# Transformer block on one core: banks, weight loads and the first cycle of a hand-written order

## The chip, the core and the metric

One core of a Trainium2 chip runs the whole program. Five engines work side by side, each through its own list of instructions in order: TensorE (PE, matmuls), VectorE (DVE), ScalarE (ACT), GpSimd (POOL) and SyncE (SP), which in this kernel only issues DMA transfers. ACT and POOL issue a few transfers too. The metric is the device time of one execution in microseconds (us). Before the change it is 1957.61 us, the median of three runs (1957.44 to 1958.38).

## The reference

The input x has 2048 tokens of 512 numbers. Two branches work on its layer norm, and their sum is added to x:

```python
def _A_ref(x, wqkv, wo):          # 32 heads of 16
    qkv = (x @ wqkv).reshape(B, S, 3, H, Dh).transpose(2, 0, 3, 1, 4)
    q, k, v = qkv[0], qkv[1], qkv[2]
    scores = jnp.einsum("bhqd,bhkd->bhqk", q, k) * (Dh ** -0.5)
    p = _softmax(scores, axis=-1)
    o = jnp.einsum("bhqk,bhkd->bhqd", p, v)
    return o.transpose(0, 2, 1, 3).reshape(B, S, D) @ wo

def _B_ref(x, w_in, w_sp, b_sp, w_out):     # F = 1792, Fh = 896
    z = _gelu(jnp.einsum("bsd,df->bsf", x, w_in))
    z1 = z[..., :Fh]
    z2 = _layernorm(z[..., Fh:], axis=-1)
    g = jnp.einsum("ts,bsf->btf", w_sp, z2) + b_sp[None, :, None]
    return jnp.einsum("bsf,fd->bsd", z1 * g, w_out)

xn = _layernorm(x)
return x + _A_ref(xn, A_wqkv, A_wo) + _B_ref(xn, B_w_in, B_w_sp, B_b_sp, B_w_out)
```

## The kernel before

**Two streams in one order.** The attention runs in 1024 steps: 16 pairs of heads, for each pair 4 chunks of 512 queries (c), for each chunk 16 tiles of 128 keys. Step n makes the scores of two heads (`scores`, L960, tile st), their exponential on ACT (`exp`, tile pf) and the product of the exponentials with v (`pv`, L934, tile o, one accumulator per chunk). 27 steps ahead of it (LEAD), the same products with the operands exchanged (`max_mm`, L650, tile mx) are reduced on DVE to row maxima (`max_red`, L658), which `max_fin` puts, through a small DRAM tile (mscr), into spare rows of the stacked q, so that the scores come out shifted. The dense products stand between: q and k of the later heads (`qk_group`), z2 (`z2_all`), z1 (`z1_all`), the spatial product (`spatial`), the output of the MLP (`mlp_out`) and of the attention (`attn_out`). Each dense matmul is done as three fp32r products of high and low parts (`mm3`, L170 to L172), so 12 of them make one product with four blocks of 128 in depth.

**The order is written by the loop at L995.** It records the instructions of all engines in program order, and no scheduler moves them. One turn is a *half*; an even half takes two steps, an odd one takes one, so two halves are a cycle of three steps. Halves below 0 hold maxima alone. In each half it records mx and st, exponentials, o products (in even halves), reductions, then one step of each generator in `bg` (loads and splits of weights) and in `side` (splits of results, the gelu and norm of z2 and z1), and last dense products from `queue`, as many as `credit` allows. Before half 0 the credit is 2600 in every half, four blocks, one product; from half 0 on it is paced by what is left to do, and only odd halves get any. `now[0]` is the half; `pool[0]` and `load` are the program's own estimate of when POOL is free and of how much ACT and DVE have.

**PSUM has eight banks.** st, mx and, at the end, al share three pairs of banks in turn (`spsum`, tags s0, s1, s2). Two single banks remain (`dpsum`): tag d (bank 7) for dense products and tag o (bank 0) for the accumulator of o. As long as no o is open, dense products may use both. In `qk_group` (L301) the two products of a call, q and k, take d and o alternately while `now[0] < -2`. A matmul that begins in a bank waits until the copy out of that bank by ACT or DVE is done: `qr` for products of q and k, `e` for o, `vall` for v.

**What follows a product of q and k.** ACT copies it out (qr), ACT makes the high part and POOL the low part (`qk_split`, tile qkhl, three buffers), and SP stores the pair of 512 KB (qscr, kscr). `load_stacks` reads them back in the layout of the scores. The normalised x (xnT) is stored too (xscr) and fetched again, group by group of 512 tokens.

**Weights of q and k.** `prepare` (L200) loads a raw tile of fp32 (three raw buffers), waits two halves, lets POOL make the parts, and only then hands them over. Heads come in four groups m of eight. The weights of m = 1 are loaded by hand at L898 to L903; those of m = 2 and 3 by `qk_prepare`, which is put into `bg` at L913, after the stacks of the first pair.

**The end.** The last pair of heads is not stored and read back like the others. `chunk_out` (L982) copies the accumulator of chunk c to SBUF (e), and `last_pair` (L776) brings values and sums of its heads into one bank (nd) with small matmuls against selector columns. For chunks 0 to 2 ACT copies nd to SBUF (L793) and `last_factors` divides there (reciprocal on DVE, product on POOL); for chunk 3 DVE divides from the bank. `last_mm` (L806) multiplies the result with the last rows of wo, two tiles of 128 tokens at a time into one pair of banks (al), and `last_add` (L814) adds that to the rest (fin, into which L772 had added the other heads' product, ao) and stores it. The last chunk's four tiles are tokens 12 to 15.

Of the kernel before, what the change touches and what calls it, by code (L numbers as in the profile page):

```python
# [16 lines left out]
P = 128  # L17
# [23 lines left out]
def fused_block(ctx, tc, x, wqkv, wo, w_in, w_spT, b_sp, w_out, out):  # L41
# [11 lines left out]

    load = {"A": 0.0, "D": 0.0}

    def act(out, in_, func, n, **kw):
        load["A"] += 0.16 + n / 1400.0
        return nc.scalar.activation(out, in_, func, **kw)  # L58

    def dve(n, rate=1):  # L60
        load["D"] += 0.065 + n / (960.0 * rate)
        return nc.vector
# [63 lines left out]
    def later(k, fn, *args):  # L126
        late.append((now[0] + k, fn, args))
# [93 lines left out]
    def prime():  # L221

        next(queue[1])
# [76 lines left out]

    def qk_group(m, g, w, tags=("d",)):  # L301
        for a in range(2):
            if now[0] < -2 and m:
                tags = ("d", "o")
            acc = dpsum(f"qk{m}_{a}_{g}", tags[a % len(tags)], ND)
            for c in range(ND):
                t = xnT[g, c]
                mm3(acc, w[a][:, 0, c * P:(c + 1) * P], w[a][:, 1, c * P:(c + 1) * P], t[:, 0, :], t[:, 1, :], c == 0, c == ND - 1)
                yield 650 + 0.5 * (c == ND - 1)
            if m == 0:  # L310
                run(qk_split(m, g, a, acc))
# [20 lines left out]
    def qk_prepare():  # L332
        yield from prepare(wq, [((m, a), *qk_weights(m, a)) for m in (2, 3) for a in range(2)])
# [81 lines left out]

    def z2_all():
        ws = w2
        def fetch(t):
            xt = piece(f"xt{t}")
            for c in range(ND):  # L420
                move(xt[:, :, c * P:(c + 1) * P], xscr[t // 4][c][:, :, (t % 4) * P:(t % 4 + 1) * P])
            return xt

        nxt = [fetch(0), fetch(1)]
        freed = []
        yield -3
        while len(ws) < 2 * ND:
            yield -1.5
        for t in range(NT):
            xt = nxt.pop(0)  # L430
            if t + 2 < NT:
                nxt.append(fetch(t + 2))
            if t == NT - 2:
                prime()
                freed.append(now[0])
                bg.append(prepare(w1, [(f, f"w1_{f}", w_in[:, f * P:(f + 1) * P], D, ND) for f in range(NF)], freed))
            z = piece(f"z2_{t}").bitcast(F32).rearrange("p a b -> p (a b)")
            for j in range(2):
# [337 lines left out]
    def last_pair(c, e):  # L776


        ones = sel["ones"]
        two = piece(f"on{c}").bitcast(F32)  # L780
        rec, on = two[:, 0, 0:P], two[:, 1, 0:P]
        acc = dpsum(f"nd{c}")
        for k in (1, 0):
            for u in range(4):
                nc.tensor.matmul(acc[32 * u:32 * u + 32, k * P:(k + 1) * P], ones[:, 0, 32 * k:32 * k + 32], e[:, u * P:(u + 1) * P], start=True, stop=True)
        yield 500.5
        if c == NG - 1:
            nc.vector.reciprocal(rec, acc[:, P:2 * P])
            nc.vector.tensor_mul(on, acc[:, 0:P], rec)
            turn.extend((4 * c + 2 * a, on) for a in range(2))  # L790
        else:
            cp = two[:, 0, P:3 * P]
            act(cp, acc[:, :2 * P], AF.Copy, 2 * P)  # L793
            bg.append(last_factors(c, cp, rec, on))
        yield 0
# [9 lines left out]

    def last_mm(t, on):  # L806

        acc = spsum(f"al{t}")
        for a in range(2):
            u = slice(32 * (t % 4 + a), 32 * (t % 4 + a) + 32)  # L810
            nc.tensor.matmul(acc[:, a, :], on[u, :], sel["ones"][u, 1, :], start=True, stop=True)
        return t, acc

    def last_add(t, acc):  # L814
        f = fin[t // 2]
        if t < NT - 2:
            dve(1024).tensor_add(f, acc, f)
            move(out[t * P:(t + 2) * P, :].rearrange("(a p) d -> p a d", p=P), f)
            return
        for a in range(2):  # L820
            dve(512).tensor_add(f[:, a, :], acc[:, a, :], f[:, a, :])
            move(out[(t + a) * P:(t + a + 1) * P, :], f[:, a, :])

    def vpack(t, h):
# [15 lines left out]
    with tc.manual_schedule(engines=engines):  # L840
# [46 lines left out]
        for g in range(NG):  # L887
            once = True
            for y in qk_group(0, g, w0, ("d", "o")):
                if y == 0 and once and g < 2:  # L890
                    once = False
                    if g == 0:
                        turn_x(1)
                        norm = norm_x(2)
                    else:
                        next(norm)
            load_stacks(0, slice(g * 512, (g + 1) * 512))
            if g == NG - 2:  # L898
                for a in range(2):
                    wq[1, a] = begin(*qk_weights(1, a))  # L900
            if g == NG - 1:
                for a in range(2):
                    wq[1, a] = end(wq[1, a])  # L903
            for t in range(4 * g, 4 * g + 4) if g else ():
                next(norm, 0)
                if t % 4 == 2:
                    if g + 1 < NG:
                        turn_x(g + 1)
                    if g + 2 < NG:
                        norm = norm_x(g + 2)  # L910
                v_tile(t, wv)
        steady.append(True)
        bg.append(qk_prepare())  # L913
        queue.extend([qk_rest(), z2_all(), z1_all(), spatial(), mlp_out(), attn_out()])
        todo = 650 * (3 * 32 + 112 + 112 + 28 * 16 + 112)
        pause = 0
# [64 lines left out]

        def chunk_out(p, c):  # L982
            e = t512(f"e{p}_{c}")
            act(e, accs.pop((p, c)), AF.Copy, 512)
            if p == NP - 1:
                later(2, lambda: urgent.append(last_pair(c, e)))
                return
            i = (p % 4) * 2
            later(1, move, escr[p // 4][c][i:i + 2].rearrange("j r w d q -> (j r w d) q"), e)
            if p % 4 == 3 or p == NP - 2:  # L990
                later(2, lambda: bg.append(norm_out(p // 4, c)))
# [3 lines left out]
        for half in range(-2 * LEAD // 3, 2 * (N // 3 + 4)):  # L995
# [3 lines left out]
            if b + LEAD >= NSTEP:  # L999
                ns = [n for n in range(b, b + 3) if n < N] if half % 2 == 0 else []  # L1000
            now[0] = half
            flush()
            for n in ns:
                if n == 16:
# [7 lines left out]
            tiles = [(scores, n) for n in ns]  # L1012
            for i, m in enumerate(ms):
                tiles.insert(1 if half % 2 == 0 else 2 * i, (max_mm, m))
            for make, n in tiles:
                make(n)
            while ended:
# [15 lines left out]
            for m in ms:  # L1033
                max_red(m)

            if half % 2 == 0:
                for m in range(ms[0] - 2, ms[0] + 1):
                    max_fin(m)
            if drain:
                drain = False  # L1040
                cost = next(queue[0], None)
                if cost is None:
                    queue.pop(0)
                else:
                    pause = -cost
            bg[:] = [g for g in bg if next(g, 0) is None]
            side[:] = [g for g in side if load["D"] > limit or next(g, 0) is None]
            ready += len(ns)
            if b < 0:
                credit = 2600  # L1050
            elif half % 2:
                credit = min(credit + 3 * (max(todo / max(DENSE - b, 10), 600 if b > DENSE - 15 else 0) if todo > 0 else max((todo + 64 * 650) / max(N - 6 - b, 8), 450)), 3250)
            else:
                continue
# [55 lines left out]
```

## Time and profile before

| | |
|---|---|
| runs, median (lowest to highest) | 1957.61 us (1957.44 to 1958.38) |
| profiled execution, its own time | 1957.17 us |
| its span, first to last instruction | 1955.4 us |
| granted TensorE clock | 0.999 |
| PE, DVE, ACT, POOL busy | 99%, 70%, 63%, 37% of the span |

In the rows of the timeline the first number is the start in us from the start of the span, the second the duration in us, then engine, line and operation, `written<-read` by the tiles' names without numbers, how many instructions are merged in the row (x4), and in brackets how long the engine was idle before and what released it. Matmuls are pipelined: a row's duration reaches past the start of the next one, so what PE spends on a matmul is read from start to start. `PEld` is the loading of weights, `SPq` the issue of a transfer by SP. A row of the waits has engine, line and what it waited for, then us in total, how many times, and the longest.

### The profile page before, as it was taken

How to read it: one execution, taken by the hardware profiler on the slowest of the kernel's cores; microseconds unless marked ns; L12 is line 12 of the kernel's file. 1: busy time of each engine (PE TensorE's matmuls, PEld its weight loads, DVE VectorE, ACT ScalarE, POOL GpSimd, SP SyncE). 2: the span in 40 equal slices, each digit the busy share in tenths (PEclk: the TensorE clock that was granted, in tenths of full speed). 3: DMA queues.
4: the chain of work that ended last, by engine and by line, in shares of the span. 5: the costliest groups of instructions: out<-in, count | busy, mean ns of one | idle time of the engine just before them, and what ended most of it. 6: DMA issues, size and time to landing. Idle time of an engine off the chain costs nothing.

```text
span 1955.4 us, 32643 instructions
## 1 busy us (share of the span) xinstructions
PE 1936.4 (99%) x12559; PEld 1050.4 (54%) x12559; DVE 1374.0 (70%) x1565; ACT 1231.1 (63%) x1407; POOL 725.1 (37%) x790
## 2 busy tenths in 40 slices
PE   9999999999999999999999999999999999999998
PEld 7765555555555555555555555555555555555543
DVE  5367777777677677777777777777777777777873
ACT  5346678888677666656666666566666655556664
POOL 3334278889776931126122531017112300002100
PEclk9999999999999999999999999999999999999999
DMA  7566344363535545365545745346454645355323
GB/s 275 198 220 182 99 115 124 114 170 114 141 130 157 181 117 139 109 154 167 137 138 166 200 134 132 104 121 205 111 156 143 174 142 136 112 145 162 105 74 113
DMA packets 229218, 284.23 MB, mean 145 GB/s; under 512 B 35192, under 2 KB 134152, under 8 KB 226184
## 3 DMA queue, kind: packets, MB, share of 16 engines
q1 hardware_dynamic: 217256, 272.64, 48.4%
q0 software_dynamic: 2592, 8.46, 1.1%
q10 hardware_dynamic: 9216, 1.05, 0.4%
q8 instruction: 99, 1.62, 0.3%
q14 instruction: 55, 0.45, 0.1%
HBM read 188.51 MB, written 93.58 MB: 144 GB/s over the span
## 4 chain that ended last, share of the span: by engine, by line
PE 93%; DVE 2%; ACT 2%; DMA 1%; issue 1%; SPq 0%; POOL 0%; DVEq 0%; ACTq 0%
PE o L934 23%; PE mx L650 16%; PE st L960 15%; PE sp L170 7%; PE sp L171 5%; PE sp L172 5%; PE qk L170 2%; PE z1p L170 2%; PE mo L170 2%; PE z2p L170 2%; PE qk L171 1%; PE qk L172 1%; PE z1p L172 1%; PE z1p L171 1%; PE mo L171 1%; PE mo L172 1%
## 5 line engine op out<-in xcount | busy, mean ns | idle before, releaser
L658 DVE TENSOR_REDUCE mm<-mx 128x2 f32<-128x1024 f32 x1024 | 1222.1, 1222 | 498.2 <-PE mx L650 493.9
L58 ACT ACTIVATE pf<-st 128x1024 f32<-128x1024 f32 x1024 | 1027.7, 1025 | 622.5 <-PE st L960 587.4
L934 PE MATMUL o<-pf,vall 128*32 128x512 f32 (+1 forms) x5120 | 511.0, 514 | 0.0
L650 PE MATMUL mx<-kst,qst 48*128 48x512 f32 x2048 | 447.5, 435 | 2.7 <-ACT pf L58 1.8
L960 PE MATMUL st<-qst,kst 50*128 50x512 f32 x2048 | 443.8, 431 | 1.3 <-DVE mm L658 1.0
L650 PEld LDWEIGHTS mx<-kst,qst 48*128 48x128 f32 x2048 | 192.2, 185 | 268.3 <-ACT pf L58 169.6
L960 PEld LDWEIGHTS st<-qst,kst 50*128 50x128 f32 x2048 | 193.2, 185 | 158.9 <-issue 85.6
L934 PEld LDWEIGHTS o<-pf,vall 128*32 128x32 f32 x5120 | 131.5, 109 | 233.3 <-issue 211.4
L170 PE MATMUL sp<-wsp,zs 128*128 128x512 f32 x448 | 194.2, 433 | 0.3 <-DVE z1i L566 0.2
L573 POOL TENSOR_TENSOR z1i<-z1i,hhl 128x512 f32<-128x512 f32 x28 | 36.0, 1286 | 413.9 <-DVE z1i L566 411.5
L171 PE MATMUL sp<-wsp,zs 128*128 128x512 f32 x448 | 176.1, 393 | 0.0
L172 PE MATMUL sp<-wsp,zs 128*128 128x512 f32 x448 | 175.8, 392 | 0.0
L170 PEld LDWEIGHTS sp<-wsp,zs 128*128 128x128 f32 x448 | 83.9, 187 | 69.4 <-issue 52.6
L172 PEld LDWEIGHTS sp<-wsp,zs 128*128 128x128 f32 x448 | 84.2, 188 | 19.5
L171 PEld LDWEIGHTS sp<-wsp,zs 128*128 128x128 f32 x448 | 84.4, 188 | 12.1
L196 POOL CAST wo<-wo0r 128x512 fp32r<-128x512 f32 x1 | 0.6, 611 | 190.1 <-DMA wo0r<-in_wo 190.1
L325 POOL TENSOR_TENSOR qkhl<-qr,qkhl 128x512 fp32r<-128x512 f32 x24 | 30.9, 1289 | 71.4 <-ACT qkhl L58 71.4
L170 PE MATMUL z2p<-w,xt 128*128 128x448 f32 x128 | 51.3, 401 | 0.0
L170 PE MATMUL mo<-wout,hp 128*128 128x512 f32 x112 | 48.6, 434 | 0.6 <-DVE xr L610 0.4
L711 POOL TENSOR_TENSOR ob<-ob 128x512 f32<-128x512 f32 (+1 forms) x16 | 20.6, 1289 | 75.6 <-DMA ob<-rscr 67.7
L172 PE MATMUL z2p<-w,xt 128*128 128x448 f32 x128 | 46.9, 366 | 0.0
L171 PE MATMUL z2p<-w,xt 128*128 128x448 f32 x128 | 46.7, 365 | 0.0
(382 smaller groups left out, 1985.2 us busy)
## 6 DMA issues: line engine op xcount, KB each, us to landing
zs<-z2scr SPq DMA_DIRECT2D x112, 512.0 KB
escr<-e SPq DMA_DIRECT2D x60, 256.0 KB
hscr<-hhl SPq DMA_DIRECT2D x28, 512.0 KB
xscr<-xnT POOLq DMA_DIRECT2D x16, 512.0 KB, 4.8
qscr<-qkhl SPq DMA_DIRECT2D x16, 512.0 KB
kscr<-qkhl SPq DMA_DIRECT2D x16, 512.0 KB
xt<-xscr SPq DMA_DIRECT2D x64, 128.0 KB
z2scr<-z2hl SPq DMA_DIRECT2D x32, 256.0 KB
```

The source lines that it names most:

```text
L58: return nc.scalar.activation(out, in_, func, **kw)
L170: nc.tensor.matmul(acc, lh, rh, start=first, stop=False)
L171: nc.tensor.matmul(acc, ll, rh, start=False, stop=False)
L172: nc.tensor.matmul(acc, lh, rl, start=False, stop=last)
L196: gps(0.6).tensor_copy(t[:, 0, :n], rw[:, :n])
L325: gps(1.3).tensor_sub(hl[:, 1 - a, :], src, hl[:, a, :].bitcast(F32))
L573: gps(1.3).tensor_add(z1, z1, hl[:, 1, :].bitcast(F32))
L650: nc.tensor.matmul(acc[:, j, :], qst[p % 2][rows, tt * P:(tt + 1) * P], kst[p % 2][rows, kc * 512:(kc + 1) * 512], start=True, stop=True)
L658: dve(1024).tensor_reduce(mmax[i // 16][:, :, t, kc], mstep.pop(i), AX.X, ALU.max)
L711: gps(1.3).tensor_mul(both[rows, 0, :], both[rows, 0, :], both[rows, 2, :])
L934: nc.tensor.matmul(acc[cols:cols + VW, a:a + w], vpack(kt - 1 + r, 2 * p + j), pf[:, j * 512 + a:j * 512 + a + w], start=(kt == 1 and a == ...
L960: nc.tensor.matmul(st[:, j, :], kst[p % 2][rows, kt * P:(kt + 1) * P], qst[p % 2][rows, c * 512:(c + 1) * 512], start=True, stop=True)
```

## The change

It has five parts.

1. **Weights.** In the last of the four turns that prepare the first pair, three steps of `qk_prepare` are taken before `load_stacks`, with the clock of halves set back by two, and three more after the last v products, with POOL's estimate reset. So loads of the weights of m = 2 and 3 are issued ahead of the last stacks, and their splits stand on POOL ahead of everything that the loop records. The generator then goes to `bg` as before.
2. **Banks of q and k.** Up to half 0, `qk_group` takes one tag for a product: o in even halves, d in odd ones.
3. **First cycle.** In the two halves of the first cycle with scores (b == 0, no o product done when the half began) the credit is 2600 as in the halves before it.
4. **Small steps on ACT.** While z2 is made (`wide` is set until its last tiles), a half in which ACT has been given more than 1.9 us by the program's estimate takes no step of `side`, unless three generators stand there. `max_fin` moves behind the queue's pending step, but only where no maxima are left, so it records nothing there.
5. **The end.** Chunk 2 is divided from its bank as chunk 3 is. The copy of the last accumulator is made in two halves of 256, ACT's and DVE's, into two tiles. The four last tiles of tokens take a bank each (two of the pairs' and banks d and o), and are added and stored one by one.

```diff
@@ def act
         load["A"] += 0.16 + n / 1400.0
+        given[0] += 0.16 + n / 1400.0
@@ def qk_group
         for a in range(2):
-            if now[0] < -2 and m:
-                tags = ("d", "o")
+            if now[0] <= 0 and m:
+                tags = ("do"[now[0] % 2 == 0],)
             acc = dpsum(f"qk{m}_{a}_{g}", tags[a % len(tags)], ND)
@@ def z2_all
         ws = w2
+        wide.append(1)
...
             if t == NT - 2:
+                wide.clear()
                 prime()
@@ def last_pair
-                nc.tensor.matmul(acc[32 * u:32 * u + 32, k * P:(k + 1) * P], ones[:, 0, 32 * k:32 * k + 32], e[:, u * P:(u + 1) * P], start=True, stop=True)
+                nc.tensor.matmul(acc[32 * u:32 * u + 32, k * P:(k + 1) * P], ones[:, 0, 32 * k:32 * k + 32], e[u // 2][:, u % 2 * P:(u % 2 + 1) * P], start=True, stop=True)
         yield 500.5
-        if c == NG - 1:
+        if c >= NG - 2:
@@ def last_mm
-        acc = spsum(f"al{t}")
+        if t < NT - 4:
+            acc = spsum(f"al{t}")
+            acc = acc[:, 0, :], acc[:, 1, :], acc
+        elif t < NT - 2:
+            acc = [spsum(f"al{t + a}")[:, 0, :] for a in range(2)]
+        else:
+            acc = [dpsum(f"al{t + a}", "od"[a]) for a in range(2)]
@@ def last_add
-        if t < NT - 2:
-            dve(1024).tensor_add(f, acc, f)
+        if t < NT - 4:
+            dve(1024).tensor_add(f, acc[2], f)
@@ before the loop
+            if g == NG - 1:
+                now[0] -= 2
+                more = qk_prepare()
+                for _ in range(3):
+                    next(more)
+                now[0] += 2
             load_stacks(0, slice(g * 512, (g + 1) * 512))
...
+        pool[0] = -1000.0
+        for _ in range(3):
+            next(more)
         steady.append(True)
-        bg.append(qk_prepare())
+        bg.append(more)
@@ def chunk_out
-            act(e, accs.pop((p, c)), AF.Copy, 512)
+            acc = accs.pop((p, c))
             if p == NP - 1:
-                later(2, lambda: urgent.append(last_pair(c, e)))
+                parts = [e[:, 0:256], e[:, 256:]]
+                if c == NG - 1:
+                    parts[1] = t512(f"e{p}_{c}b")[:, 0:256]
+                    act(parts[0], acc[:, 0:256], AF.Copy, 256)
+                    dve(256).tensor_copy(parts[1], acc[:, 256:])
+                else:
+                    act(e, acc, AF.Copy, 512)
+                later(2, lambda: urgent.append(last_pair(c, parts)))
                 return
+            act(e, acc, AF.Copy, 512)
@@ the loop
             now[0] = half
+            given[0] = 0.0
...
+            fresh = done == 0
             for make, n in tiles:
...
-            side[:] = [g for g in side if load["D"] > limit or next(g, 0) is None]
+            side[:] = [g for g in side if load["D"] > limit or wide and given[0] > 1.9 and len(side) < 3 or next(g, 0) is None]
             ready += len(ns)
-            if b < 0:
+            if b < 0 or b == 0 and fresh and not done:
                 credit = 2600
```

More of the change, by code (lines that the diff above doesn't have):

```diff
@@ L54, in fused_block @@
     load = {"A": 0.0, "D": 0.0}
+    wide = []
+    given = [0.0]
     def act(out, in_, func, n, **kw):
         load["A"] += 0.16 + n / 1400.0
+        given[0] += 0.16 + n / 1400.0
         return nc.scalar.activation(out, in_, func, **kw)
@@ L806, in last_mm @@
     def last_mm(t, on):
-        acc = spsum(f"al{t}")
+        if t < NT - 4:
[5 more added lines that the diff above has]
+            acc = [dpsum(f"al{t + a}", "od"[a]) for a in range(2)]
         for a in range(2):
             u = slice(32 * (t % 4 + a), 32 * (t % 4 + a) + 32)
-            nc.tensor.matmul(acc[:, a, :], on[u, :], sel["ones"][u, 1, :], start=True, stop=True)
+            nc.tensor.matmul(acc[a], on[u, :], sel["ones"][u, 1, :], start=True, stop=True)
         return t, acc
@@ L820, in last_add @@
         for a in range(2):
-            dve(512).tensor_add(f[:, a, :], acc[:, a, :], f[:, a, :])
+            dve(512).tensor_add(f[:, a, :], acc[a], f[:, a, :])
             move(out[(t + a) * P:(t + a + 1) * P, :], f[:, a, :])
@@ L1034, in fused_block @@
                 max_red(m)
-            if half % 2 == 0:
-                for m in range(ms[0] - 2, ms[0] + 1):
+            closing = range(ms[0] - 2, ms[0] + 1) if half % 2 == 0 else ()
+            if b + LEAD < NSTEP:
+                for m in closing:
                     max_fin(m)
@@ L1045, in fused_block @@
                     pause = -cost
+            if b + LEAD >= NSTEP:
+                for m in closing:
+                    max_fin(m)
             bg[:] = [g for g in bg if next(g, 0) is None]
-            side[:] = [g for g in side if load["D"] > limit or next(g, 0) is None]
+            side[:] = [g for g in side if load["D"] > limit or wide and given[0] > 1.9 and len(side) < 3 or next(g, 0) is None]
             ready += len(ns)
-            if b < 0:
+            if b < 0 or b == 0 and fresh and not done:
                 credit = 2600
```

## The prediction

> **What bounds the kernel now.** I read the page first, then the timeline of TensorE (PE) at the places that the diff names, then the waits of PE in two windows, and last the timeline of the end.
>
> ```profile
> span 1955.4 us, 32643 instructions
> PE 1936.4 (99%) x12559; PEld 1050.4 (54%) x12559; DVE 1374.0 (70%) x1565; ACT 1231.1 (63%) x1407; POOL 725.1 (37%) x790
> PE 93%; DVE 2%; ACT 2%; DMA 1%; issue 1%; SPq 0%; POOL 0%; DVEq 0%; ACTq 0%
> ```
>
> PE is busy from end to end and carries 93% of the chain of waits. The change leaves its 12,559 matmuls as they are, so time can come only from three things: stops of PE, the price of going from one kind of matmul to another, and the tail behind the last matmul. The profiled execution took 1957.17 us, 1.77 more than its span; the median of the runs is 1957.61. I sum changes against the profiled execution and add the sum to the median.
>
> **Weights ahead, first products.** Where the maxima (mx) begin, one product of 12 matmuls stands between every two groups of mx:
>
> ```profile
> 83.78 0.60 ACT L58 ACTIVATE vall<-v 128x512 f32<-128x512 f32 x1 [2.12 <-PE v L172]
> 84.11 0.50 PE L170 MATMUL qk<-xnT,wqk 128*128 128x512 f32 x1
> ...
> 86.73 0.39 PE L172 MATMUL qk<-xnT,wqk 128*128 128x512 f32 x1
> 87.05 0.73 PE L650 MATMUL mx<-kst,qst 48*128 48x512 f32 x4
> 87.71 0.50 PE L170 MATMUL qk<-xnT,wqk 128*128 128x512 f32 x1
> 88.05 0.39 PE L171 MATMUL qk<-xnT,wqk 128*128 128x512 f32 x1
> 88.28 0.39 PE L172 MATMUL qk<-xnT,wqk 128*128 128x512 f32 x1
> ...
> 92.51 0.49 PE L650 MATMUL mx<-kst,qst 48*128 48x512 f32 x2 [0.88 <-DVE mm L658]
> ```
>
> At 92.51 PE stops, because the weights of q and k group 2 were not ready, no product stood between the mx, and four of these in a row caught up with VectorE's reductions. The weights were late because SyncE (SP) issued their loads last:
>
> ```profile
> 74.92 2.52 SPq L102 DMA_DIRECT2D qst<-qscr  x2
> 79.19 0.77 SPq L102 DMA_DIRECT2D kst<-kscr  x2
> 82.19 0.40 SPq L102 DMA_DIRECT2D wqk_0r<-in_wqkv  x1
> ```
>
> ```profile
> 85.39 0.61 POOL L196 CAST wqk<-wqk_0r 128x512 fp32r<-128x512 f32 x1 [15.52 <-DMA wqk_0r<-in_wqkv]
> ```
>
> Issued at about 75, some 7 us earlier, three of the four reach an idle GpSimd (POOL) at about 78 (85.39 less 82.19 is 3.2 us of landing). Their issues (3 x 0.4) go past eight loads of stacks, but fall where SP waited between 77.4 and 79.2, so these lose nothing. The four POOL pairs are then done before the products need them, and the early fetch of normalised x finds buffers long free. The stop goes: **-0.9**.
>
> The new choice of bank puts the first product (qk1_0_0) into the bank that the last v product has just left; before it had the other. It must wait for the copy that ends at 83.78 + 0.60 = 84.38, plus some 0.05 of handover and 0.1 for a first weight load that is not ahead, against a start at 84.11: **+0.4**. Only products queue behind it.
>
> **Products in the first cycle with scores.** Before, scores (st) and mx start alone:
>
> ```profile
> 138.22 0.50 PE L960 MATMUL st<-qst,kst 50*128 50x512 f32 x2
> 138.78 1.94 ACT L58 ACTIVATE pf<-st 128x1024 f32<-128x1024 f32 x2 [1.02 <-PE st L960]
> 138.79 0.40 PE L960 MATMUL st<-qst,kst 50*128 50x512 f32 x2
> 139.86 0.49 PE L650 MATMUL mx<-kst,qst 48*128 48x512 f32 x2 [0.67 <-ACT pf L58]
> 140.28 0.50 PE L960 MATMUL st<-qst,kst 50*128 50x512 f32 x2
> 140.61 0.60 ACT L58 ACTIVATE qr<-qk 128x512 f32<-128x512 f32 x1
> ...
> 141.26 0.50 PE L170 MATMUL qk<-xnT__1212,wqk 128*128 128x512 f32 x1
> ```
>
> Six pairs take 3.04 us (138.22 to 141.26). With no wait they follow each other at 0.23 to 0.33, some 1.6 in all. A product behind st1 gives ScalarE (ACT) its time, and this loss goes: **-1.4**.
>
> But the variable with the bank's tag is set only in halves up to 0. The second product of that pair (qk1_1_3, half 1) keeps the tag of the first, and both take bank 0, which is also the only bank of o. In the recorded order PE runs st0, mx27, st1, qk1_0_3, mx28, st2, mx29, qk1_1_3, st3, mx30, st4, o0_0; ACT runs pf0, pf1, two steps of an older product, pf2, qr1_0_3, one split, pf3, pf4, qr1_1_3. So qk1_1_3 waits for qr1_0_3, behind pf2: st2 + 0.56 (138.22 to 138.78) + 0.97 (half of 1.94) + 0.60 + 0.05 = 2.2 us after st2, instead of mx29 and a switch, 0.55: **+1.6**. Then o0_0 waits for qr1_1_3, behind pf3 and pf4: st3 + 0.56 + 1.94 + 0.60, less 0.1 of overlap, about 3.05, instead of three intervals, 0.87: **+2.2**. Behind qk1_1_3 stand st3, mx30 and st4, so ACT and VectorE idle too. Nothing covers these two.
>
> **Switches.** PE's order now has 357 runs of dense products instead of 353 (many of 12 became 6 and 9). The rows from 86.73 to 88.28 price one run: 0.32 instead of 0.23 into mx, 0.33 instead of 0.23 out of it, 0.34 instead of 0.23 to the second matmul, some 0.28 in all. Four more: **+1.1**.
>
> **ACT's small steps held back.** While z2 is made, halves with over 1.9 us given to ACT postpone them, unless three generators wait. First the waits of PE from 205 to 420, then from 420 to 530:
>
> ```profile
> PE mx L650 <- ACT pf L58: 0.4, 2, 0.2
> PE st L960 <- DVE mm L658: 0.2, 1, 0.2
> ```
>
> ```profile
> PE mx L650 <- ACT pf L58: 0.8, 4, 0.2
> PE st L960 <- DVE mm L658: 0.2, 1, 0.2
> ```
>
> ```profile
> 424.74 0.40 PE L960 MATMUL st<-qst,kst 50*128 50x512 f32 x2
> 424.97 0.39 PE L650 MATMUL mx<-kst,qst 48*128 48x512 f32 x2
> ...
> 429.73 0.40 PE L960 MATMUL st<-qst,kst 50*128 50x512 f32 x2
> 430.30 0.50 PE L650 MATMUL mx<-kst,qst 48*128 48x512 f32 x2 [0.17 <-ACT pf L58]
> ```
>
> Eight stops. One costs more than its row: 430.30 less 429.73 is 0.57 instead of 0.23, so 0.34, and 0.1 at the next switch, 3.6 for all. More than that the rule cannot bring; at worst it delays z2 steps and adds as many stops as half of these, +1.8. In the recorded order 33 of the 67 small steps stand in two-exponential halves before and after, so inside z2 I expect little. But five of the eight stops fall where the last z2 tiles' steps meet z1's, and there the new order spreads them: I take **-2.0**. Four z1 products now finish on VectorE and one no longer does, three more net on an engine 70% busy: nothing.
>
> **The tail.**
>
> ```profile
> 1934.75 0.39 ACT L58 ACTIVATE on<-nd 128x256 f32<-128x256 f32 x1
> 1935.19 0.50 PE L170 MATMUL ao<-wo,op 128*128 128x512 f32 x1 [1.50 <-ACT on L58]
> 1942.55 1.13 PE L811 MATMUL al<-sel,on 32*128 32x512 f32 x4
> 1944.74 0.60 ACT L58 ACTIVATE e<-o 128x512 f32<-128x512 f32 x1 [2.42 <-PE o L934]
> 1945.39 0.65 PE L785 MATMUL nd<-e,sel 128*32 128x128 f32 x16 [0.72 <-ACT e L58]
> 1946.10 0.96 DVE L788 RECIPROCAL on<-nd 128x128 f32<-128x128 f32 x1 [1.15 <-PE nd L785]
> 1948.70 1.23 DVE L817 TENSOR_TENSOR fin<-al,fin 128x1024 f32<-128x1024 f32 x1 [0.18 <-PE al L811]
> 1949.84 1.28 DVE L821 TENSOR_TENSOR fin<-al,fin 128x512 f32<-128x512 f32 x2
> ```
>
> The copy of nd2 stood behind exponentials and held the last ao product 1.50. VectorE, idle there, now reads the bank itself, and the hold goes (-1.5). The second al of that chunk moves ahead of the last o products (+1.1), and the weight loads are ahead again (-0.4): the last o ends 0.8 earlier. The copy of e is halved between ACT and VectorE, but the recorded order makes VectorE wait for ACT: 0.39 (ACT's 256 columns) + 0.05 + VectorE's 256 columns, not in this trace, between 0.29 and 0.69 by its nearest rows; 0.4 as 256 lies near the 128 end. That is 0.25 more than 0.60, of which the first nd matmuls cover 0.1. The add of 1024 that stood ahead of the last ones is done by then, and four adds of 0.65 replace 1.23 + 1.28, starting after two matmuls instead of four: 0.35 earlier. Together **-1.0** for the last add; the stores behind it keep their distance.
>
> [...]
>
> **Sum.** -0.9 + 0.4 - 1.4 + 1.6 + 2.2 + 1.1 - 2.0 - 1.0 = 0.0: **1957.6 us**.
>
> **The rivals.** *A, the bank waits only take the place of later ones* (faster). While PE stands at qk1_1_3 and o0_0, ACT and VectorE catch up, and stops of the following cycles fall away. Then 3.8 goes out of the sum and with it z2's remaining 1.6 of stops: 1952.2; with half of that, 1954.9. For it: ACT is in time again after them. Against: ACT and VectorE idle there as well.
>
> *B, a store holds ACT at the first scores* (slower). ACT's splits wait for the stores that free their buffers:
>
> ```profile
> 121.83 0.53 SPq L102 DMA_DIRECT2D kscr<-qkhl  x1
> ```
>
> ```profile
> 129.85 0.63 ACT L58 ACTIVATE qkhl<-qr 128x512 fp32r<-128x512 f32 x1 [4.89 <-DMA kscr<-qkhl]
> ```
>
> That store, issued behind four fetches of x, landed after 8.0 us. The changed order has the same constellation for kscr1_1_2, issued at about 135.6, and ACT wants its buffer at 144.0, ahead of pf0. Two us of slack are left; from 10 us of landing on every us more delays pf0 and the two bank waits. At 14.5 it costs 4.5: 1962.1. Against: 8.0 was with as much traffic.
>
> *C, the weights come no earlier*: 0.9 stays, 1958.5.
>
> **Chances.** Forecast 0.58 (its own range 1954.5 to 1960.3: z2 at both ends, 0.9 either way elsewhere), A 0.20, B 0.15, C 0.07. A measurement of this kernel tells about 0.2% (3.9 us) from no change. A ends below 1953.7 in three cases of four (0.15), the forecast in one of twenty (0.03): faster 0.18. B ends above 1961.5 in most (0.13), the forecast in 0.02: slower 0.15. Same 0.67. The range reaches into A and B: 1953.0 to 1961.2.
>
> **What would show it.** Right: no stop at mx6; PE stopped at qk1_1_3 and o0_0, released by ACT's qr, 1.3 to 2 us each by their rows; no wait of ao for ACT's copy at the end; VectorE's copy of e behind ACT's. Wrong: stops of PE in z2 that grow or vanish altogether, ACT waiting for DMA ahead of pf0, or a last add whose distance to the end changes.

## The result, and the profile after

| | before | after |
|---|---|---|
| runs, median (lowest to highest) | 1957.71 us (1957.44 to 1958.83, 6 runs) | 1970.74 us (1966.43 to 1975.65, 6 runs) |
| profiled execution, its own time | 1957.17 us | 1975.65 us |
| its span | 1955.4 us | 1973.8 us |
| granted TensorE clock | 0.999 | 0.994 |

The ratio is 1.0067, with a 95% interval from 1.0056 to 1.0078: the change makes the kernel 13 us slower, and the forecast of 1957.6 (1953.0 to 1961.2) was wrong. Two things beside the median are new. The runs lie 9 us apart, where those of before lie 1.4 apart. And the granted clock of the profiled execution is 0.994 instead of 0.999.

From the page of the profile after, the head, the row of the clock in 40 slices, and the shares of the chain of waits:

```profile
span 1973.8 us, 32650 instructions
PEclk9999999999999999998999999999999999999999
PE 82%; DMA 4%; DVE 2%; POOL 2%; ACT 1%; issue 1%; SPq 1%; DVEq 0%; ACTq 0%; POOLq 0%
```

The chain went through PE for 93% of the span before; now parts of it go through DMA and POOL. That is the first hint that late loads have got on the path. The waits of PE over the whole span (us, times, longest) name two kinds of stop:

```profile
PE mx L656 <- ACT pf L62: 3.8, 6, 2.3
PE mo L174 <- DMA hp<-hscr: 2.2, 2, 1.1
PE o L955 <- ACT qr L62: 2.0, 1, 2.0
...
PE qk L174 <- ACT qr L62: 1.4, 1, 1.4
```

The last two are the bank waits of the forecast (1.4 and 2.0 us); the first two, for ACT's exponentials and for loads of h, are not in it. The place of the bank waits in the timeline of PE, and what comes behind them:

```profile
151.90 0.40 PE L656 MATMUL mx<-kst,qst 48*128 48x512 f32 x2
153.66 0.50 PE L174 MATMUL qk<-xnT__1350,wqk 128*128 128x512 f32 x1 [1.37 <-ACT qr L62]
...
157.18 0.40 PE L981 MATMUL st<-qst,kst 50*128 50x512 f32 x2
159.63 1.06 PE L955 MATMUL o<-pf,vall 128*32 128x512 f32 x8 [2.04 <-ACT qr L62]
...
163.64 0.63 PE L174 MATMUL qk<-xnT__1352,wqk 128*128 128x512 f32 x1
164.07 0.63 PE L175 MATMUL qk<-xnT__1352,wqk 128*128 128x512 f32 x1
...
169.63 0.40 PE L175 MATMUL qk<-xnT__1354,wqk 128*128 128x512 f32 x1
169.87 0.40 PE L176 MATMUL qk<-xnT__1354,wqk 128*128 128x512 f32 x1
```

At 163.64 a matmul of q and k starts 0.43 us ahead of the next one; at 169.63 it is 0.24, about half that. The views by windows (the last three numbers of a row are granted clock, DMA share, GB/s) say why, here and at a second place near 900:

```profile
150.00:160.00 10.00, 6.59 (x35) 4.09 (x37) 3.58 (x3) 5.97 (x9) 4.22 (x4) 1.00 0.49 159
160.00:168.00 8.00, 8.00 (x38) 3.92 (x34) 4.00 (x7) 3.25 (x4) 7.32 (x9) 0.57 0.12 31
168.00:178.00 10.00, 10.00 (x74) 5.62 (x63) 6.33 (x8) 5.50 (x7) 1.81 (x2) 1.00 0.34 93
...
898.00:908.00 10.00, 9.76 (x37) 4.91 (x39) 3.58 (x3) 3.75 (x5) 9.68 (x12) 0.50 0.81 241
```

PE counts as busy, but its clock is halved: from 160 to 168 the mean is 0.57, from 898 to 908 it is 0.50. So a stop cost its own length here and then half of a slow stretch behind it. The second place begins with a stop of 2.3 us by its row; the timeline of all engines there:

```profile
887.05 0.68 DVE L572 SCALAR_TENSOR_TENSOR z1i<-sp,z1i 128x512 f32<-128x512 f32 x1
887.84 0.61 POOL L200 CAST wsp<-wsp_5r 128x512 fp32r<-128x512 f32 x1 [3.63 <-DMA wsp_5r<-in_w_spT]
...
891.23 1.94 ACT L62 ACTIVATE pf<-st 128x1024 f32<-128x1024 f32 x2 [1.90 <-PE st L981]
893.41 0.61 POOL L200 CAST wsp<-wsp_7r 128x512 fp32r<-128x512 f32 x1 [1.68 <-DMA wsp_7r<-in_w_spT]
895.35 1.27 POOL L579 TENSOR_TENSOR z1i<-z1i,hhl 128x512 f32<-128x512 f32 x1
...
896.65 0.63 ACT L62 ACTIVATE hhl<-z1i 128x512 fp32r<-128x512 f32 x1 [3.49 <-POOL z1i L579]
897.19 1.92 ACT L62 ACTIVATE pf<-st 128x1024 f32<-128x1024 f32 x2
...
898.24 0.80 PE L656 MATMUL mx<-kst,qst 48*128 48x512 f32 x2 [2.31 <-ACT pf L62]
```

Read it backwards. PE's mx waits for an exponential (pf); that stands on ACT behind the split of h (hhl), which waited 3.49 us for POOL's z1i; that stands on POOL behind the splits of spatial weights, which waited 3.63 and 1.68 us for loads (wsp_5r, wsp_7r). VectorE had z1i ready at 887.73 (887.05 + 0.68), 7.6 us before POOL came to it. Every engine keeps its recorded order in these rows, and so late loads hold up three of them. In the kernel before, the same step waited for VectorE alone (waits of POOL, 885 to 900):

```profile
POOL z1i L573 <- DVE z1i L566: 2.7, 1, 2.7
```

Two things on SP's queue stand ahead of these loads. First, its issues for a new group of spatial weights (wsp) are mixed with those of the next pair's stacks (qst, kst):

```profile
857.31 0.90 SPq L106 DMA_DIRECT2D qst<-qscr  x2
858.25 0.42 SPq L106 DMA_DIRECT2D wsp_1r<-in_w_spT  x1
858.72 1.70 SPq L106 DMA_DIRECT2D kst<-kscr  x2
...
869.06 0.35 SPq L106 DMA_DIRECT2D wsp_3r<-in_w_spT  x1
869.51 1.59 SPq L106 DMA_DIRECT2D kst<-kscr  x2
```

Second, before it issued wsp_5r at 884.51, SP stood 7.0 us until the small store of the row maxima (mscr) had landed (waits of SP, 855 to 900):

```profile
SPq L106 <- DMA mscr<-ms: 7.0, 1, 7.0
```

In the kernel before, SP waits for that store too (3.7 us up to 890.31), but by then it has issued the weights up to wsp_8r, and only those up to wsp_7r stand ahead of z1i on POOL.

The change touches none of these transfers. What it moved is the dense order: 18 products of q and k are made before the first scores instead of 15, and two more in the first cycle. z2 then begins at score 23 instead of 44, and the spatial stage 15 scores earlier. The scores at which each spatial group starts, by the recorded order of the two kernels (loads of stacks are asked for at 14 + 64 k, those of a group's weights from the last product of the group before on):

```
                      group 0   weights of 1   group 1   group 2   group 3
before                  299         407          425       551       680
after                   284         395          413       545       674
stacks asked for        270         398          398       526       654
```

Before, the weights of group 1 were asked for 9 scores after the stacks; after, 3 scores before them. The lead is 15 scores at the start of the stage and 12, 6 and 6 at the later groups.

### The profile page after: what moved, and what is told of

It reads as the page before. It is cut to its first block, busy times and chain, and to the rows that moved or that the text cites. A ratio compares the mean times of both kernels' runs of the same rounds, so it can differ in the third digit from the quotient of the medians.

```text
span 1973.8 us, 32650 instructions
## 1 busy us (share of the span) xinstructions
PE 1947.9 (99%) x12559; PEld 1053.0 (53%) x12559; DVE 1378.6 (70%) x1571; ACT 1233.1 (62%) x1406; POOL 719.2 (36%) x783
## 4 chain that ended last, share of the span: by engine, by line
PE 82%; DMA 4%; DVE 2%; POOL 2%; ACT 1%; issue 1%; SPq 1%; DVEq 0%; ACTq 0%; POOLq 0%
PE o L955 22%; PE st L981 14%; PE mx L656 14%; PE sp L174 7%; PE sp L176 5%; PE sp L175 5%; PE z1p L174 2%; PE mo L174 2%; PE z2p L174 1%; DVE mm L664 1%; PE z1p L175 1%; PE z1p L176 1%; PE mo L176 1%; PE mo L175 1%; PE z2p L176 1%; PE z2p L175 1%
```

## The experiments

Theory: (1) the two bank waits cost their own length and a slow stretch of the clock; (2) the early products move the dense order ahead, by 15 scores at the start of the spatial stage, which puts the loads of spatial weights on top of those of the stacks. Rivals: the stops alone count; the loss is in the early weights, the hold-back or the tail; the stops are only moved. Every ratio below is against runs of the kernel before on the same chip, whose median was 1957.27 to 1957.92.

**e1_again.** The changed kernel once more.

> The changed kernel once more, for a second profile. Theory (two long stops of TensorE, each followed by some 8.5 us at about half the granted clock): the stops at qk1_1_3 (1.4 us) and o0_0 (2.0 us) near 155 and the slow stretch from 159.6 to 168.4 are there again, because the order of instructions makes them. The stop of 2.3 us at mx444 near 898 hangs on when a load of the spatial weights lands; if it belongs to the change it is there again, if it was chance of that execution it is gone and the time is 6 to 7 us less than the first profile's 1975.65, about 1968 to 1969. Rival (the 13 us lie spread over the whole kernel): the same total with other stops.

1970.52 us (1967.18 to 1974.67), ratio 1.0074 (1.0059 to 1.0090). The profiled execution, 1967.18, stops at qk1_1_3 and o0_0 as the first did (1.4 and 2.0), with a slow stretch from 159.6 to 163.0 (3.4 us; by the clock's records that of the first execution lasts 6.8, not the 8.5 of the expectation). At 893 ACT waited only 1.2 us for POOL, PE did not stop, and the clock stayed full. So the stop there hangs on the execution, and so does the length of the slow stretch. Both add to the spread of the runs; that they make all of it is not shown.

**e2_banks.** The second product of the first cycle takes bank d.

```diff
-            if now[0] <= 0 and m:
+            if now[0] <= 1 and m:
                 tags = ("do"[now[0] % 2 == 0],)
```

> Only the bank of one product differs from the changed kernel: qk1_1_3 takes bank d, so it waits for no younger copy, and o0_0 waits only for qr1_0_3, which is done by then. Theory (stop plus clock): both stops go (3.5 us) and with them the slow stretch after them (some 4 us): 7 to 8 us less, 1962 to 1964, granted clock 1.00 from 150 to 200. Rival 1 (stops alone count, the slow clock comes in any case): 3.5 less, 1967. Rival 2 (the stops only move to the next products or exponentials): 0 to 1 less, 1970.

1966.71 us (1963.50 to 1969.99), ratio 1.0048 (1.0035 to 1.0060). Both stops and the slow stretch are gone from the profile. The difference, 3.8, is near rival 1; but this kernel's profile has a stop of 2.1 near 893 with 3.4 us at half clock, and its runs lie 6.5 apart, so this pair does not settle what the stretch costs (e12 bears on it).

**e3_nofirst.** No products in the first cycle.

```diff
-            if b < 0 or b == 0 and fresh and not done:
+            if b < 0:
```

> The changed kernel without dense products in the first cycle with scores. Theory (stop plus clock): no product shares the bank of o, so both stops and the slow stretch go (7 to 8 us less), the six pairs at the start of the scores stop again for 1.4 us, and the dense order has fewer switches (1.6 less by the intervals of the kernel before): 1962 to 1964. Rival (the order of all dense work, shifted by the early products, costs the time through late loads in the spatial stage): then the time depends on the new order, and the stop near 898 is what goes: 1963 as well, but with the slow stretch at 160 still there. The profile tells them apart.

1963.78 us (1961.67 to 1967.67), ratio 1.0035 (1.0022 to 1.0049). As the theory says, no bank stop; the clock from 145 to 155 is 1.00. As the rival says, a stop in the spatial stage with half clock behind, 2.2 near 673 (its spatial groups start at 287, 416, 545 and 674). A stop of 1.6 at 1673, for a load of h in the output of the MLP, has a slow stretch too. Both halves of the theory are needed.

**e4_nohold.** No hold-back of small ACT steps.

```diff
-side[:] = [g for g in side if load["D"] > limit or wide and given[0] > 1.9 and len(side) < 3 or next(g, 0) is None]
+side[:] = [g for g in side if load["D"] > limit or next(g, 0) is None]
```

> The changed kernel without the hold-back of small ACT steps during z2. Theory (the hold-back does nearly nothing): excess between 200 and 500 within 1 us of the changed kernel, time 1969 to 1972. Rival (as predicted, it saves 2.0 there): 2 us more, 1973. Second rival (the held steps make POOL and its loads late later on): the stop near 898 goes, 6 to 7 us less, 1964.

1968.68 us (1966.34 to 1971.70), ratio 1.0059 (1.0045 to 1.0073): below e1 rather than above, but within its spread. The hold-back saves nothing here and is not the cause.

**e5_banks_stacks.** e2_banks, with the loads of stacks 12 scores earlier.

```diff
-                if n % 64 == 14 and n // 64 + 1 < NP:
+                if n % 64 == 2 and n // 64 + 1 < NP:
                     load_stacks(n // 64 + 1)
```

> The kernel of e2_banks (1966.71) with the loads of the next pair's stacks asked for 12 scores earlier (n % 64 == 2 instead of 14); TensorE's order is the same. Theory (the early products moved the dense order 15 to 21 scores ahead, so the loading of the spatial weights for a new group now falls on the loads of the stacks, POOL gets its weights late, ACT's step behind POOL is late and the exponentials behind that): the stops at the starts of the groups (640, 674, 893, 1128) go, with the slow stretches behind them: 1958.5 to 1961, and the runs lie within 3 us of each other instead of 6.5. Rival (the stops belong to the dense order itself or to the scratch loads, not to the stacks): 1965 to 1967 with stops at the same places.

1961.98 us (1959.48 to 1964.92), ratio 1.0022 (1.0014 to 1.0031): 4.7 less than e2, just above the theory's range, and its runs lie 5.4 apart, not within 3. The stops near 893 and 1128 are gone, but not because the loads are on time: from 860 to 905, with no load of stacks near, POOL waits 8.6 us for wsp_7r, which SP issued behind 7.2 us of waiting for the store of maxima (mscr). ACT does not wait for POOL there. So the stacks are a part of the cause and not the whole. At the start of the stage PE's stop is 3.0 in this profile, where e2's had 0.8. The waits from 625 to 645:

```profile
POOL wsp L200 <- DMA wsp_2r<-in_w_spT: 4.5, 1, 4.5
DVE os L709 <- POOL os L707: 3.9, 1, 3.9
PE st L981 <- DVE mm L664: 3.0, 1, 3.0
```

A like chain on another engine: a sum of the softmax sums (os) stands on POOL behind the late weight, VectorE waits for it, and the reductions of the maxima behind it on VectorE hold PE for 3.0 us.

**e6_before_late.** The kernel before with the stacks 12 scores later (`n % 64 == 26`).

> The kernel before with one number changed: the loads of the next pair's stacks are asked for 12 scores later (n % 64 == 26), so that they meet the loads of the spatial weights as they do in the changed kernel; TensorE's order is that of before. Theory (meeting of the two groups of loads): stops of 1 to 2.5 us at st429 and at the starts of the other groups, some with a slow stretch: 1960 to 1967, and runs that differ by several us. Rival (only the shifted dense order matters): 1957 to 1958.5, no new stops in the spatial stage.

1977.24 us (1975.86 to 1983.18), ratio 1.0105 (1.0091 to 1.0119): slow as expected, for another reason. Its waits of PE:

```profile
PE ao L170 <- DMA op<-oscr: 5.5, 1, 5.5
PE mx L650 <- DMA kst<-kscr: 4.4, 3, 2.7
PE mx L650 <- ACT pf L58: 3.9, 8, 2.2
```

The stacks came too late for the maxima themselves, and there was no stop at the start of group 1. The time says nothing about the theory, and the missing stop speaks against "any meeting of the two loads will do". A test that leaves the stacks where they were was needed: e11.

**e7_before_tail.** The kernel before with part 5 of the change alone.

> The kernel before with the last part of the change alone (last but one sums divided from their bank, last tokens singly, copy of the last sums halved). My sum gave it -1.0: 1956.3. Rival (the halved copy and the single adds cost what the wait of the last ao product saves): 1957.3, no change. Second rival: the last tokens' new banks wait for VectorE: 1958.

1956.95 us (1955.63 to 1957.60), ratio 0.9996 (0.9987 to 1.0005). From the timeline of PE, the last matmul before the tail where both kernels still do the same, in before and in e7, and then the end of e7's timeline:

```profile
1906.46 0.50 PE L170 MATMUL ao<-wo,op 128*128 128x512 f32 x1 [0.45 <-ACT on L58]
```

```profile
1906.02 0.50 PE L170 MATMUL ao<-wo,op 128*128 128x512 f32 x1 [0.45 <-ACT on L58]
...
1943.64 0.38 ACT L58 ACTIVATE e<-o 128x256 f32<-128x256 f32 x1 [1.23 <-PE o L940]
1944.06 0.43 DVE L996 COPY e_3b<-o 128x256 f32<-128x256 f32 x1 [2.46 <-ACT e L58]
...
1945.21 0.96 DVE L788 RECIPROCAL on<-nd 128x128 f32<-128x128 f32 x1 [0.73 <-PE nd L785]
...
1946.64 1.14 PE L817 MATMUL al<-sel,on 32*128 32x512 f32 x8 [1.48 <-DVE on L789]
1947.77 2.48 DVE L827 TENSOR_TENSOR fin<-al,fin 128x512 f32<-128x512 f32 x4 [1.27 <-PE al L817]
```

From that matmul to the end of the last add it is 44.23 (1947.77 + 2.48 less 1906.02), and 44.66 in the kernel before (1949.84 + 1.28 less 1906.46): 0.43 less, as the medians say, though the interval of the ratio includes no difference. The tail is no cause of the loss.

**e8_before_hold.** The kernel before with part 4 alone.

> The kernel before with the hold-back of small ACT steps alone. My sum gave it -2.0: 1955.3. Theory after e4_nohold (it moves the stops of z2 without removing any): 1957 to 1958. Rival (it makes POOL's work late): 1958.5 or more.

1956.88 us (1956.25 to 1957.62), ratio 0.9997 (0.9988 to 1.0006): at most a small gain, nothing like 2.0.

**e9_banks_dve.** e2_banks with the two POOL steps of the chains on VectorE.

```diff
-        gps(1.3).tensor_add(z1, z1, hl[:, 1, :].bitcast(F32))
-        yield from pool_done()
+        dve(512).tensor_add(z1, z1, hl[:, 1, :].bitcast(F32))
+        yield
...
-        gps(0.2).tensor_add(sums[rows, 0, :], sums[rows, 0, :], sums[rows, 1, :])
+        dve(32).tensor_add(sums[rows, 0, :], sums[rows, 0, :], sums[rows, 1, :])
```

> The kernel of e2_banks (1966.71) with two small steps moved from POOL to VectorE: the sum ahead of ACT's split of h (z1i) and the first sum of the softmax sums (os). TensorE's order is the same. Theory (POOL waits at a cast for a spatial weight that has not landed, and the step behind it in POOL's order holds ACT or VectorE, which hold TensorE): the stops at st272, mx444 and mx576 go, as ACT and VectorE wait for POOL no more: 1958 to 1961. Rival (TensorE itself comes for the weights too early): stops at the sp products instead, 1964 to 1967. Second rival (VectorE is the next bound): stops of mx and st for VectorE all through the spatial stage, 1966 or more.

1963.12 us (1962.60 to 1964.77), ratio 1.0030 (1.0019 to 1.0040), and the runs lie within 2.2. From 860 to 905:

```profile
ACT pf L62 <- PE st L981: 16.6, 15, 2.0
POOL wsp L200 <- DMA wsp_3r<-in_w_spT: 5.2, 1, 5.2
```

POOL waits 5.2 us for a weight, and ACT does not wait for POOL. The long stops at the groups' starts and the slow clock are gone, so the chain through POOL was the way. The time is 2 above the theory's range: small stops of PE for VectorE (2.4 in 8) and one of 1.1 at 658 are left, and the rest stays open.

**e10_banks_phase.** e2_banks, with the pace up to score 250 aimed 62 scores later. Its groups start at 299, 425, 551 and 680, as before; z2 still begins early, at score 26.

```diff
-max(todo / max(DENSE - b, 10), ...
+max(todo / max(DENSE + (62 if b < 250 else 0) - b, 10), ...
```

> The kernel of e2_banks with one number: the pace of the dense work up to score 250 aims at 62 scores later, so that the spatial groups start at scores 299, 425, 551 and 680, as in the kernel before, instead of 284, 413, 545 and 674. Theory (the place of the dense order against the loads of stacks and maxima made the late loads): no stops at the groups' starts, and what is left are the change's small gains and costs: 1955.5 to 1958, runs within 2 us of each other. Rival (the early weights or the first products cost time in another way): 1961 or more with the stops still there.

1958.53 us (1958.00 to 1961.40), ratio 1.0006 (0.9997 to 1.0014): 8.2 less than e2, by one number that alters nothing but when dense products come. Its waits from 860 to 905:

```profile
ACT pf L62 <- PE st L981: 17.1, 15, 1.9
...
POOL wsp L200 <- DMA wsp_7r<-in_w_spT: 4.2, 1, 4.2
```

POOL still waits for a load, but nothing that ACT wants stands behind it at that time, and neither ACT nor PE waits for POOL.

**e11_before_early.** The opposite: the kernel before with `DENSE - (55 if b < 250 else 0)`. Its groups start at 284, 413, 542 and 674.

> The kernel before with the opposite: the pace up to score 250 aims at 55 scores earlier, so that the spatial groups start at scores 284, 413, 542 and 674, as in the changed kernel. Nothing else of the change is in it. Theory (place of the dense order): stops at the starts of the groups (st272, mx444, mx576), slow stretches in some runs, 1960 to 1967 and runs that differ by several us. Rival: 1957 to 1958.5, no such stops.

1972.96 us (1967.26 to 1975.09), ratio 1.0069 (1.0057 to 1.0082). None of the change's edits is in it, and it has a loss as large, the spread and the chain. It is not a copy of the changed kernel: its group 2 starts 3 scores earlier, and its longest stop, 3.8 at 1127, is 1.0 in e1. So it shows that a moved order can cost this much by itself, not that it costs so much in the changed kernel. Its waits from 1105 to 1130:

```profile
ACT hhl L58 <- POOL z1i L573: 5.5, 1, 5.5
...
POOL wsp L196 <- DMA wsp_2r<-in_w_spT: 4.8, 1, 4.8
PE mx L650 <- ACT pf L58: 3.8, 1, 3.8
```

**e12_phase.** The changed kernel with the pace of e10, and so e10 with the changed kernel's banks.

> The changed kernel with the pace of e10_banks_phase and its own banks, so that it differs from e10_banks_phase only in the bank of qk1_1_3. Theory (each of the two stops there costs its own time, 3.5 together, and a slow stretch after the second 2 to 4 more): 5 to 7.5 us above e10_banks_phase. Rival (the stops alone): 3.5 above. Second rival (taken back later): under 2 above.

1964.86 us (1963.26 to 1966.69), ratio 1.0034 (1.0022 to 1.0046): 6.3 above e10, within the theory's 5 to 7.5. The stops are 3.5 of it (1.4 and 2.1 beyond the usual intervals). The profiled execution is the fastest of these runs (1963.26) and shows no slow stretch behind them; the row of o0_0, and then the view by windows:

```profile
158.80 1.06 PE L955 MATMUL o<-pf,vall 128*32 128x512 f32 x8 [2.04 <-ACT qr L62]
```

```profile
160.00:168.00 8.00, 8.00 (x52) 4.25 (x50) 6.67 (x11) 4.30 (x5) 7.41 (x9) 1.00 0.11 33
```

52 matmuls start there instead of 38. So the stretch comes in some executions and not in others; after, e1 and e4 had it for 6.8, 3.4 and 3.4 us, which cost half of that. The other four runs of e12 have no profile, but their granted clock falls as their time rises, from 0.998 at 1963.26 to 0.996 at 1966.69: 0.002 of 1962 us is 3.9 (the clocks are rounded to 0.001), and the times differ by 3.4.

**e13_phase_nohold.** e10 without the hold-back.

> The kernel of e10_banks_phase (1958.53) without the hold-back of small ACT steps. Theory (in the changed order the hold-back lets the steps pile up until a third generator waits, and then they come together ahead of exponentials: the three stops at 259, 271 and 277): the excess from 250 to 300 falls from 4.3 to 1 to 2 and the time by 2 to 3: 1955.5 to 1956.5, below the kernel before. Rival (these stops belong to the slower pace in z2): no change, 1958.5. Second rival (the hold-back saves 0.5 as in e8_before_hold): 1959.

1957.41 us (1955.73 to 1959.25), ratio 1.0001 (0.9992 to 1.0010). Waits of PE from 250 to 285, first e10, then e13:

```profile
PE st L981 <- DVE mm L664: 1.0, 3, 0.4
PE mx L656 <- ACT pf L62: 0.9, 1, 0.9
```

```profile
PE st L981 <- DVE mm L664: 0.2, 1, 0.2
```

In these two profiles the stops that the hold-back was to remove are made by it. The 1.1 between the medians is less than the 2 to 3 expected; against each one's own runs of before it is 0.6, and the intervals overlap.

**e14_tail_hold.** The kernel before with parts 4 and 5 only.

> The kernel before with the two parts that cost nothing by themselves, the tail (-0.4 in e7_before_tail) and the hold-back (-0.5 in e8_before_hold), and none of the early weights and products. If the two add up: 0.9 below the kernel before of the same runs, 1956.5 to 1957. Rival (both differences were noise): 1957.4 to 1957.9.

1955.45 us (1954.98 to 1957.95), ratio 0.9991 (0.9982 to 1.0000). It is 15 us faster than the changed kernel; against the kernel before it is 2.0 less, with an interval that just reaches no difference. That is more than the 0.9 expected, and nothing here shows why. It is the best version found.

The two causes together, medians in us:

| | bank of qk1_1_3 as changed | bank d |
|---|---|---|
| dense order as changed | 1970.5 (e1) | 1966.7 (e2) |
| groups start where they did before | 1964.9 (e12) | 1958.5 (e10) |

The bank costs 3.8 or 6.3, the order 5.7 or 8.2, depending on whether the other is there; together 12.0. (The two rows ran on two chips; against their own runs of before, 0.65 apart, the order costs 6.3 or 8.8.) Without both, what is left of the change is about as fast as the kernel before.

## Why the prediction was wrong

**Right, and of the size said.** The stop at mx6 is gone, so rival C is out. qk1_0_0 waits (0.42 beyond its usual interval, 0.4 said). The loss at the start of the scores is gone. qk1_1_3 and o0_0 wait for ACT's qr, 1.37 and 2.04 by their rows; 1.6 and 2.2 were said. No stop before pf0 for a store, so rival B is out. VectorE's copy of e stands behind ACT's and takes 0.43 (0.4 said). In the tail, counted from the matmul shown under e7, ACT's last copy starts 37.62 after it instead of 38.28 (0.7 earlier, 0.8 said) and the reciprocal 39.19 instead of 39.64, so that 0.2 is lost to the halved copy (0.15 said).

**The step that failed: "Switches".** The forecast took the changed order of PE as 357 runs of dense products instead of 353 and priced the switches, +1.1. That the order stands elsewhere against everything which goes by scores was not asked. Three products more before the scores, and two in their first cycle, put z2 21 scores ahead and the spatial stage 15, and with them the loads that they ask for; the stacks and the maxima stayed where they were. e11 shows that this costs time by itself (+15.0 against its runs of before), e10 takes it away from e2 (-8.2). How much of it is due to the loads of stacks and how much to SP's wait for the store of maxima, no run separates. No rival had it.

**The term that was too small: the two bank waits.** 3.8 was their length alone. The 6.3 between e12 and e10 holds 3.5 of stops; the rest fits the slow clock behind them, as the rows of after show it and the granted clocks of e12's runs bear out, though the profiled execution of e12 itself had none.

**The term that did not come: z2.** -2.0 was forecast; e8 gives -0.5, and in the changed order e10 and e13 have it at +0.6 against their runs of before. Neither is told from nothing, so even its sign is open. In the profiles, holding steps back moves the stops (1.9 from 250 to 285 in e10, 0.2 in e13).

**The tail, -1.0, measured -0.4.** What did not come is the 0.35 for the single adds: from the start of the reciprocal to the end of the last add it is 5.04 (1950.25 less 1945.21), and 5.02 before (1951.12 less 1946.10). The forecast let the first add begin after two matmuls of al instead of four. But in e7's trace the eight matmuls of al start in two groups of four, at 1946.64 to 1946.66 and 1947.15 to 1947.20, and each tile's last one is in the second group.

**Rival A** (the bank waits only take the place of later ones) is refuted by e12 against e10.

**What is left over.** Without the 3.8 of the bank waits the forecast's terms give 3.8 below the kernel before; e10, without them and with the groups in place, is 0.6 above. Of these 4.4 us, 2.6 are z2 and 0.6 the tail, by their medians; 1.2 stay open.

## What to carry to other kernels

When products are moved in a kernel whose other streams are timed by something else, list at which step of each stream the big groups of loads now fall, before pricing a single stop: here the unchanged loads cost more than every edited line (the order 5.7 or 8.2 us, the bank 3.8 or 6.3). A step that another engine waits for should not stand behind a step that waits for a load (here z1i, ready at 887.73, was taken up by POOL 7.6 us later, behind splits that had waited 3.63 and 1.68 for loads); the chain from load to POOL to ACT to PE is read from the waits of the engines that are *not* the bottleneck, SP's queue among them. And a stop of TensorE is to be priced with the clock behind it: here 13 of 14 stops of 1.55 us and more had 3.4 to 10.2 us at half clock behind them, as the next section shows.

## What was not expected of the hardware

The granted clock. For every stop of PE between 100 and 1900 us that was over 1.1 us longer than the usual interval, this is the length (us) and behind it the time at half clock that the trace's clock records show from there on:

```
after   1.4: 0    2.1: 6.8   2.5: 10.2   1.2: 0   1.2: 0
e1      1.4: 0    2.1: 3.4   1.2: 0
e2      2.3: 3.4
e3      2.4: 3.4  1.2: 0     1.7: 3.4    1.2: 0
e4      1.4: 0    2.1: 3.4   1.2: 0
e5      3.2: 6.8
e6      1.5: 0    3.0: 3.4   1.3: 0      2.3: 3.4   5.6: 6.8
e11     1.1: 0    1.3: 0     1.55: 3.4   4.0: 3.4
e12     1.4: 0    2.1: 0
```

Of 14 stops of 1.55 and more, 13 were followed by 3.4, 6.8 or 10.2 us at half clock; of the shorter ones none was. In before, e7, e8, e9 and e10 no stop was that long, and the clock was full: 1.00 by one record from 7.76 to 1949.94 in before, and 1.00 in every window from 0 to 1950 in the other four. In e13 and e14 the mean over the span is 0.998, as in e12. (The lengths are start to start, less the median interval of the same pair of matmuls in the kernel before.)

In after, the records have 0.50 for 6.83 us from 160.56 on, 0.93 after the stop at o0_0 ended (159.63), and for 10.24 us from 897.84 on, 0.40 before the stop there ended (898.24). The odd one of the 14 is the stop at o0_0 in e12. By its row it is as long as in after, 2.04, but the clock is 1.00 in the windows from 150 to 178, where after has 0.57 from 160 to 168. What sets it apart was not shown, nor why a stretch lasted 3.4 us in one case and 6.8 or 10.2 in another.
